# First two attention units in float32, their scales and 16-bit operands made later

## The chip, the cores and the metric

The kernel runs on one core of a Trainium2 chip. The metric is the device time of one launch in microseconds, the median of repeated runs. Five engines work side by side on the core, each through its own queue in program order: PE (TensorE, the matmuls), DVE (VectorE), ACT (ScalarE), POOL (GpSimd) and SP (SyncE, which here issues nearly all DMA transfers). They meet only through semaphores.

## The reference, cut to what matters

One transformer block with adaptive layer norm, for 2048 rows of width 512: attention with 32 query heads over 8 key and value heads of which the last 512 keys count, and then a gated feed-forward part of width 1792.

```
mod = (silu(c) @ w_mod)                                # six vectors of 512: sa, ca, ga, sb, cb, gb
h = layernorm(x) * (1 + ca) + sa
q = h @ wq                                             # 2048 x 4096, 32 heads of 128
scores = q @ k.T * 128 ** -0.5                         # 512 keys per head
o = softmax(scores) @ v
x = x + ga * (o @ wo)
h = layernorm(x) * (1 + cb) + sb
x = x + gb * ((gelu(h @ w_gate) * (h @ w_up)) @ w_down)
```

All inputs and the output are float32.

## The kernel before

**Number format.** A product of two float32 matrices is made by `mm3` (line 90) from 16-bit halves: each operand is scaled into the range of float16 and split into a high half and the low rest, and three matmuls (low by high, high by high, high by low) add up in one bank of PSUM. Each operand therefore needs a scale, which comes from norms: `sumsq` (line 218, ACT) squares a tile, `sums` (line 222, PE) adds over partitions, `norm2` takes a root on POOL (line 235), and a reciprocal on DVE closes it. `halves` (lines 158 and 159) makes high and low half on POOL, `times` (line 162) scales on POOL; `split_post` (lines 746 and 747) makes the high half on ACT and the low half on DVE.

**Units and slots.** The attention is cut into units: one head and one block of 512 queries. A unit has four slots, one for 128 queries each. In slot t the program writes, in this order: the scores of slot t on PE (`scores`, into one of two PSUM banks `ps`), their maximum on DVE (`peak`, line 989, tile `nm`), what is filed under ("e", t), the low halves of the probabilities of slot t-3 on DVE (`low`, line 1015) with their transposing DMA on SP (line 1019, `pt<-p`), what is filed under ("d", t), the exponential on ACT (`expo`, line 998, tile `ee`), the high halves of slot t-2 on ACT (line 1010), what is filed under ("x", t), then a number of tasks from a work list on PE, then what is filed under t, and what is filed under ("w", t). `at` files a step under such a key, `then` files it some slots later under ("d", ...). So a slot is a place in each queue and no time: an engine that waits in one slot holds back all that it has in later ones. In the first eight slots the number of tasks is given by hand (`EARLY`: 2, 2, 0, 0, 2, 2, 0, 0), later it is three.

**The first units.** Units 0 and 1 are heads 0 and 1 with query block 0, units 2 and 3 the same heads with block 1, and unit 4 is head 2 with block 0. Unit u's queries q are made by tasks in the slots of unit u-1 (`q_plain`, four groups of three matmuls), the probabilities of unit u meet v in the slots of unit u+2 (`pv_tasks`, tile `po`). The tasks for q of unit 4 stand at slot 12; they need the weights of pair 1 and the halves of query block 0.

**Before slot 0.** `begin` does the layer norm of the first 512 rows, makes the modulation vectors (`mod_col` on DVE, line 137, and matmuls with one column, line 1030, tile `mps`), and then the scales: `mod_scale` for the modulation vectors, `w_first` and `w_spread` for the weights of the first pair, `k_spread` for k. With these scaled vectors (`cols`) it turns the first block on PE (`ln_out`'s `turn`, line 439, tile `pln`), makes the scaled tile `hf` on DVE (line 185), sends it to DRAM (`hs<-hf`), and makes the high half on ACT (line 450) and the low half on POOL or DVE (line 454). It splits the weights (`high_w`, line 1057, `low_w`, line 1060) and k (`split_post`), and runs the q of unit 0 with matmuls on dummy data between (`q_first` and `warm`, lines 1067 and 1091). The norm statistics of the second block (`nb`, line 392) come partly in `begin`, partly in slots 0 and 1; the second block is turned in slot 2, with `hf` on DVE, high halves on ACT and low halves on POOL in slots 2 to 4.

**On POOL in slots 3 to 17.** In program order: the norm of v (line 235, `vmax`), v's halves (slot 6), the scales of weight pair 1 (`lw` to `ksc`, slots 6 to 8), its two weight tiles (`plain_steps`, slots 8 and 9), k of pair 1 (slot 10), the scales of the attention output (`ysc`, slot 12), four differences for a later block scheme (`combos`, line 581, slots 13 to 16), the product `gs` (slot 15), and the norm of the second k head (`kmax`, slot 15). DVE takes the reciprocal of that last one (line 250, `kinv`) in slot 17, ahead of the maximum of slot 18.

Of the kernel before, what the change touches and what calls it, by code (L numbers as in the profile page):

```python
# [18 lines left out]
P = 128  # L19
S, D, F = 2048, 512, 1792  # L20
HQ, HKV, DH = 32, 8, 128
W = 512
# [36 lines left out]
SETPOS = (20, 14, 13, 12, 10, 8)  # L59
SETPOS2 = (18, 12, 11, 10, 9, 7)  # L60
TAIL = 12


@with_exitstack
def block_kernel(ctx: ExitStack, tc: tile.TileContext, x, kT, v, wq, wo, wg, wu, wd, cT, wc, wm, out):
# [8 lines left out]
    def tmp(name):  # L74
        return pool.tile([P, 512], F32, tag="e", name=name, bufs=NE)
# [129 lines left out]
    def mod_scale(j, name, const_, m=None, mid=nop, between=nop):  # L205
        m, g, s = m or mod_max(j), little("mg", 2, 1), little("ms", 1, 1)
        everywhere(g, m, 2, False)
        mid()
        nc.vector.tensor_tensor(s, g[:, 0:1], g[:, 1:2], op=ALU.add)
        ts(s, s, FLOOR, RT / TOP13, ALU.max)  # L210
        ts(col(name), s, const_)
        between()
        nc.vector.reciprocal(s, s)
        ts(cols[:, j:j + 2, :], cols[:, j:j + 2, :], s)

    def sumsq(out, src):
        with nc.allow_low_precision(reason="only a scale follows from it, which the margin in norm2 covers"):
# [211 lines left out]
    def ln_out(qb, dt):  # L429
        name = (("b11", "b21"), ("y", "b22"))[qb][dt // 2]  # L430
        p = dt % 2
        st = {}

        def turn():
            st["ps"] = bank("acc", "pln", NACC)
            for i in range(QT):
                if qb and dt == 0 and i > 1:
                    fill(4)
                nc.tensor.transpose(st["ps"][:, i * P:(i + 1) * P], xn[qb * QT + i][:, dt * P:(dt + 1) * P], ident)

        def affine(act=True):
            st["f"] = pool.tile([P, D], F32, tag="ot", name="hf", bufs=NOT) if qb else tmp("hf")
            if act:
                nc.scalar.activation(st["f"], st["ps"], AF.Identity, scale=cols[:, 1, dt:dt + 1], bias=cols[:, 0, dt:dt + 1])
            else:
                ts(st["f"], st["ps"], cols[:, 1, dt:dt + 1], cols[:, 0, dt:dt + 1], op1=ALU.add)
            dma(spilled(0, qb)[:, dt, :], st["f"])

        def direct():
            nc.scalar.activation(block(0, name)[:, p, :], st["ps"], AF.Identity, scale=cols[:, 1, dt:dt + 1], bias=cols[:, 0, dt:dt + 1])  # L450

# [4 lines left out]
        return turn, affine, low, direct  # L456

    xn = {}
    waits_ = []

    def put_off(n, fn):
# [223 lines left out]
    def k_items(pr):  # L685
        g = pr // 2
        st, load = reader(kT[g])
        m = {}

        def stat():  # L690
# [12 lines left out]

        return (load, stat, spread, parts) + ((m,) if pr == 0 else ())
# [81 lines left out]
            5: ("s1", "t1"), 6: ("s2", "t2"), 7: ("s3", "t3")}  # L786
    SET, RAW = {}, {}

    def set_load(key, srcs, only=None):
        for k, src in enumerate(srcs):  # L790
            if only in (None, k):
                t = pool.tile([P, 512], F32, tag="rw", name="rw", bufs=NRW)
                dma(t, src)
                RAW.setdefault(key, {})[k] = t

# [124 lines left out]
    def q_plain(u):  # L920
# [10 lines left out]

        return [(lambda kt=kt: group(kt), (lambda: q_post(u, st["p"])) if kt == KT - 1 else None) for kt in range(KT)]

    def pv_tasks(u):
# [43 lines left out]
    def scores(t):  # L978
        u, i = divmod(t, 4)
        half, pr, qb, h = units[u]  # L980
        k = KV[half, pr, 0]
        sl = slice(i * P, (i + 1) * P)
        ps = bank("s", "ps", 2)
        mm3(ps, qT[u][:, 0, sl], qT[u][:, 1, sl], k[:, 0, :], k[:, 1, :], True, True, left=True)
        E[t] = {"ps": ps}

    def peak(t):
# [71 lines left out]
    def low_w(k):  # L1059
        nc.vector.scalar_tensor_tensor(SET[0][k][:, 1, :], RAW[0][k], col("wsc", 0), SET[0][k][:, 0, :], op0=ALU.mult, op1=ALU.subtract)  # L1060

    def q_first(warm):
        ps = bank("acc", "pq", NACC)
        for term, (a, b) in enumerate(((0, 0), (1, 0), (0, 2))):
            for kt in range(KT):
                w, m, p = SET[0][0], BK[0, ("b11", "b21")[kt // 2]], kt % 2
                nc.tensor.matmul(ps, w[:, a, kt * P:(kt + 1) * P], m[:, b + p, :], start=term + kt == 0, stop=term == 2 and kt == KT - 1)
            if term == 0:
                warm(3)
        q_post(0, ps)  # L1070

    def begin():
        now[0] = -1
        for i in range(QT):
            na[i][0]()
            na[i][1]()
        na[2][2]()
        na[3][2]()
        na[0][2]()
        na[1][2]()  # L1080
        na[2][3]()
        na[3][3]()
# [4 lines left out]
        wps = bank("s", "warm", 2)  # L1087

        def warm(n):
            for _ in range(n):  # L1090
                nc.tensor.matmul(wps, junk[:, 0:P], junk, start=True, stop=True)
# [8 lines left out]
        k0[1]()  # L1100
        ts(cols[:, 1, :], cols[:, 1, :], 1.0, None, ALU.add)
        ts(cols[:, 0, :], mps[:, 0:KT], 1.0, None, ALU.mult)
        pst = {}

        def mid():
            o0[0][0]()
            pst["w"] = sums(m["m"], 2)
            o0[1][0]()
            pst["k"] = sums(k0[4]["m"], 1)
            o0[2][0]()  # L1110
            o0[3][0]()

        mod_scale(0, "ma", SCALE * TOP13 * TOP13, mod_max(0), mid)
        w = w_first(m["m"], pst["w"])
        o0[0][1](False)
        inv_k = k0[2](False, pst["k"])
        nc.vector.reciprocal(col("wsc", 0), w)
        inv_t, last = w_spread(0, m["m"], w)
        o0[0][3]()
        high_w(0)  # L1120
        for n in range(1, KT):
            o0[n][1](False)
            o0[n][3]()
            if n == 1:
                o0[0][2](nc.gpsimd)
            if n == 2:
                inv_k()
                inv_t()
                last()
        warm(4)  # L1130
        low_w(0)
        o0[1][2]()
        o0[2][2](nc.gpsimd)
        low_k = k0[3](True)
        o0[3][2]()
        low_k()
        nb[0][0]()
        nb[0][1]()
        high_w(1)
        q_first(warm)  # L1140
        v0[1]()
        run(("e", 0))
        run(("d", 0))
        low_w(1)


    at(0, nb[0][2], nb[0][3], nb[1][0], nb[1][1], nb[2][0], nb[2][1])
# [69 lines left out]
    for g in range(NG):  # L1217
# [5 lines left out]
        spread = None if half else lambda m, pr=pr: w_spread(pr, m)  # L1223
        if 0 < g < GW:
            a, b = plain_steps(g, by)
            sched_pair(g, srcs, t0 - (19 if g > 1 else 13), spread, [(t0 - (13 if g > 1 else 8), a)], [(t0 - (11 if g > 1 else 7), b)])
# [306 lines left out]
    def pushes(u, y):  # L1533
# [305 lines left out]
```

## Time and profile before

| | us |
|---|---|
| median of 3 runs | 1733.64 (1733.24 to 1734.52) |
| the profiled execution, its own time | 1736.03 |
| its span, first to last instruction | 1734.2 |
| PE busy in the span | 1710.5 (99%) |
| DVE, ACT, POOL busy | 1430.4, 1254.9, 1093.9 |
| maximum of slot 0 (DVE) begins | 26.94 |
| maximum of slot 4 begins | 39.18 |
| maximum of slot 18 begins | 71.66 |

Times within the profile count from the start of the span. A row of the timeline gives the start, the time from the start of its first instruction to the end of its last one, the engine, the line, the operation, the tiles (written<-read), shapes and the number of instructions; in brackets stands how long the engine had been idle before it and what ended that. Matmuls follow each other faster than one lasts, so three in a row with 0.81 are not three times 0.27. A busy PE at the page's 99% includes the time in which one matmul runs out.

### The profile page before, as it was taken

To read this page: it belongs to the slowest core of one execution; us is meant where nothing else is said; L and a number is where in the kernel's file an instruction comes from. 1 tells how busy PE (TensorE), PEld (TensorE's weight loads), DVE (VectorE), ACT (ScalarE), POOL (GpSimd) and SP (SyncE) were. 2 spreads that over 40 slices of the span, in tenths; PEclk is the share of its full clock that TensorE was granted. 3 is DMA by queue.
4 is the path that set the end of the run, shared out by engine and by line. 5 is a ranking of instruction groups with operands and counts; after the bars stand their busy time and mean duration, and the time that the engine had idled before them with its cause. 6 is when DMAs were issued, how large, how long until landed. Compare 5 with 4: busy or idle time off the path is not lost.

```text
span 1734.2 us, 26336 instructions
## 1 busy us (share of the span) xinstructions
PE 1710.5 (99%) x8012; PEld 786.3 (45%) x8012; DVE 1430.4 (82%) x2476; ACT 1254.9 (72%) x2819; POOL 1093.9 (63%) x1328
## 2 busy tenths in 40 slices
PE   7999999999999999999999999999999999999998
PEld 4444444444444444444444444444444444444444
DVE  7898898888888899887788888888896788666666
ACT  5988788888888777897788777787785354455442
POOL 4889778777788884655665755747760346735424
PEclk9999999999999999999999999999999999999999
DMA  7999999999999988999999999999997556365353
GB/s 232 222 197 212 219 213 204 226 203 216 215 230 223 208 203 187 217 205 226 197 232 224 200 232 208 201 223 219 225 228 161 164 147 199 110 167 170 96 157 103
DMA packets 693454, 343.51 MB, mean 198 GB/s; under 512 B 579136, under 2 KB 602688, under 8 KB 693312
## 3 DMA queue, kind: packets, MB, share of 16 engines
q1 hardware_dynamic: 693024, 341.30, 85.7%
q8 instruction: 63, 1.03, 0.2%
q14 instruction: 79, 0.65, 0.1%
q10 hardware_dynamic: 288, 0.52, 0.1%
HBM read 137.50 MB, written 63.70 MB: 116 GB/s over the span
## 4 chain that ended last, share of the span: by engine, by line
PE 88%; DVE 4%; ACT 4%; DMA 2%; POOL 1%; issue 1%; SPq 0%; DVEq 0%; POOLq 0%; ACTq 0%
PE py L90 18%; PE po L90 17%; PE ps L90 17%; PE fa L90 8%; PE qa L90 8%; PE fc L90 4%; PE qc L90 4%; PE ya L90 3%; PE fb L90 2%; PE qb L90 2%; PE yc L90 2%; DMA pt<-p 1%; ACT ee L998 1%; ACT p L1010 1%; DVE nm L989 1%; PE pq L90 1%
## 5 line engine op out<-in xcount | busy, mean ns | idle before, releaser
L998 ACT ACTIVATE ee<-ps,nm 128x512 f32<-128x512 f32 x512 | 349.7, 683 | 186.1 <-DVE nm L989 181.0
L1015 DVE SCALAR_TENSOR_TENSOR p<-ee,rr,p 128x512 f16<-128x512 f32 x512 | 456.7, 892 | 6.2 <-ACT p L1010 5.8
L989 DVE TENSOR_REDUCE nm<-ps 128x1 f32<-128x512 f32 x512 | 350.1, 684 | 106.6 <-PE ps L90 104.0
L90 PE MATMUL ps<-k,qt 128*128 128x512 f16 x1536 | 414.8, 379 | 5.3 <-ACT ee L998 4.1
L1010 ACT ACTIVATE p<-ee,rr 128x512 f16<-128x512 f32 x512 | 364.5, 712 | 21.0 <-DMA pt<-p 10.0
L90 PE MATMUL po<-pt,v 128*128 128x512 f16 x1536 | 373.0, 379 | 2.8 <-DMA pt<-p 1.8
L90 PE MATMUL py<-wo,ot 128*128 128x512 f16 x1536 | 371.5, 379 | 0.0
L90 PEld LDWEIGHTS <-w 128*128 128x128 f16 x2184 | 213.4, 98 | 258.8 <-issue 0.8
L90 PEld LDWEIGHTS <-v 128*128 128x128 f16 x1536 | 149.8, 98 | 185.5 <-DMA pt<-p 3.5
L90 PEld LDWEIGHTS <-ot 128*128 128x128 f16 x1536 | 150.2, 98 | 181.7 <-DVE ot L747 0.5
L90 PEld LDWEIGHTS <-qt 128*128 128x128 f16 x1536 | 145.7, 98 | 176.4 <-issue 5.0
L1319 POOL TENSOR_TENSOR fg<-fg 128x512 f32<-128x512 f32 x48 | 62.9, 1310 | 148.5 <-DVE fg L1293 145.6
L747 DVE SCALAR_TENSOR_TENSOR ot<-po,ot 128x512 f16<-128x512 f32 x128 | 87.7, 685 | 37.5 <-ACT ot L746 37.0
L1303 ACT ACTIVATE at<-fg 128x512 f16<-128x512 f32 x92 | 56.4, 626 | 83.7 <-DVE fg L1293 63.6
L998 ACT ACTIVATION_READ_ACCUMULATOR ee<-ps,nm 128x1 f32 x512 | 99.9, 195 | 0.0
L959 DVE SCALAR_TENSOR_TENSOR acc<-py,ysc,acc 128x512 f32<-128x512 f32 x128 | 94.6, 739 | 5.3 <-PE py L90 5.3
L90 PE MATMUL qa<-t,w 128*128 128x512 f16 x348 | 84.9, 379 | 0.0
L235 POOL TENSOR_TENSOR lw<-lw,half__86 128x1 f32<-128x1 f32 x39 | 24.0, 616 | 92.4 <-DVE lw L185 92.4
L90 PE MATMUL fa<-t,w 128*128 128x512 f16 x336 | 81.6, 379 | 0.0
L746 ACT ACTIVATE ot<-po 128x512 f16<-128x512 f32 x128 | 73.7, 576 | 5.0 <-PE po L90 5.0
L90 PEld LDWEIGHTS <-wo 128*128 128x128 f16 x504 | 49.3, 98 | 61.0 <-issue 2.0
L90 PE MATMUL ya<-at,wo 128*128 128x512 f16 x288 | 76.0, 379 | 0.9 <-DVE yt L1686 0.7
(243 smaller groups left out, 2765.5 us busy)
## 6 DMA issues: line engine op xcount, KB each, us to landing
w<-kept SPq DMA_DIRECT2D x123, 256.0 KB, 3.4
wo<-kept SPq DMA_DIRECT2D x72, 256.0 KB, 3.3
kept<-stage SPq DMA_DIRECT2D x67, 256.0 KB, 3.3
raw<-in_wo SPq DMA_DIRECT2D x56, 256.0 KB, 3.2
kept<-w SPq DMA_DIRECT2D x39, 256.0 KB, 3.4
rw<-in_wq SPq DMA_DIRECT2D x38, 256.0 KB, 3.1
hs<-hf SPq DMA_DIRECT2D x32, 256.0 KB, 2.8
pt<-p SPq DMA_TRANSPOSE x512, 3.5
```

The costliest lines, as they stand in the source:

```text
L90: nc.tensor.matmul(ps, a, b, start=first and n == 0, stop=last and n == 2, skip_group_check=chain)
L235: nc.gpsimd.tensor_tensor(out, out, half_, op=ALU.pow)
L746: nc.scalar.activation(t[:, 0, :], src, AF.Copy, scale=scale)
L747: return lambda: nc.vector.scalar_tensor_tensor(t[:, 1, :], src, scale, t[:, 0, :], op0=ALU.mult, op1=ALU.subtract)
L959: nc.vector.scalar_tensor_tensor(acc[ti], st["p"], by, acc[ti], op0=ALU.mult, op1=ALU.add)
L989: nc.vector.tensor_reduce(nm, E[t]["ps"], axis=AX.X, op=ALU.max, negate=True)
L998: nc.scalar.activation(e, E[t]["ps"], AF.Exp, bias=E[t]["nm"], scale=1.0, accum_out=sm[:, t % 2:t % 2 + 1])
L1010: nc.scalar.activation(p16[:, 0, :], E[t]["e"], AF.Copy, scale=E[t]["r"])
L1015: nc.vector.scalar_tensor_tensor(p16[:, 1, :], E[t]["e"], E[t]["r"], p16[:, 0, :], op0=ALU.mult, op1=ALU.subtract)
L1303: nc.scalar.activation(t[:, 0, :], g, AF.Copy)
L1319: nc.gpsimd.tensor_tensor(g[o], g[a], g[b], op=ALU.subtract)
```

## The change

- `q_full` replaces `q_first` for unit 0 and `q_plain` for unit 1: four float32 matmuls of 128x512 each from the weight tile as loaded (`RAW[0]`) and the unscaled `hf` tiles of the first block, kept in `HF`. ACT copies the result into one float32 tile with the factor 128 ** -0.5.
- `scores` of units 0 and 1 (`NFULL = 2`, slots 0 to 7) is one float32 matmul with the k tile as loaded.
- `begin` no longer makes any scale or half. It turns the first block, makes `hf` on DVE and ACT by turns, takes the statistics of three tiles of the second block, and runs q of unit 0. The dummy matmuls of `warm` go.
- The scales (`mod_scale`, `w_first`, `k_spread`, `w_spread`) are made in slots 0 to 2; the halves of the first weights in slots 1 to 3 (ACT high, DVE low), those of k in slots 4 and 5.
- The first block's `hf` are multiplied by the scale on POOL and sent to DRAM in slots 4 and 5 (`scaled`); their high and low halves are made on POOL in slots 5, 7, 8 and 9 (`both`).
- Loads move: pair 1's weights are loaded in slot 1 into the tag "wo"; the loads of two of the four tiles for the first `combos` group move from slots 1 and 2 to slots 7 and 8.

```diff
+NFULL = 2
...
         def affine(act=True):
-            st["f"] = pool.tile([P, D], F32, tag="ot", name="hf", bufs=NOT) if qb else tmp("hf")
+            st["f"] = pool.tile([P, D], F32, tag="ot", name="hf", bufs=NOT)
...
+            if qb:
+                dma(spilled(0, qb)[:, dt, :], st["f"])
+            else:
+                HF[dt] = st["f"]
+
+        def scaled(by):
+            times(st["f"], by)
             dma(spilled(0, qb)[:, dt, :], st["f"])
+
+        def both():
+            t = block(0, name)
+            nc.gpsimd.tensor_scalar(t[:, p, :], st["f"], 1.0, 1.0, op0=ALU.mult, op1=ALU.mult)
+            nc.gpsimd.tensor_tensor(t[:, 2 + p, :], st["f"], t[:, p, :], op=ALU.subtract)
...
+    def q_full(u):
+        st = {}
+
+        def group(kt):
+            if kt == 0:
+                st["p"] = bank("acc", "pq", NACC)
+            nc.tensor.matmul(st["p"], RAW[0][u][:, kt * P:(kt + 1) * P], HF[kt], start=kt == 0, stop=kt == KT - 1)
+
+        def post():
+            qT[u] = pool.tile([P, QB], F32, tag="qt", name="qf", bufs=3)
+            nc.scalar.activation(qT[u], st["p"], AF.Copy, scale=SCALE)
...
     def scores(t):
...
-        mm3(ps, qT[u][:, 0, sl], qT[u][:, 1, sl], k[:, 0, :], k[:, 1, :], True, True, left=True)
+        if u < NFULL:
+            nc.tensor.matmul(ps, qT[u][:, sl], KV["raw"], start=True, stop=True)
+        else:
+            k = KV[half, pr, 0]
+            mm3(ps, qT[u][:, 0, sl], qT[u][:, 1, sl], k[:, 0, :], k[:, 1, :], True, True, left=True)
...
     def begin():
...
+        for n in range(KT):
+            o0[n][0]()
+            o0[n][1](n % 2 == 1)
+        for i in range(3):
+            nb[i][0]()
+            nb[i][1]()
+        mm = mod_max(0)
+        k0[1]()
         v0[1]()
-        run(("e", 0))
-        run(("d", 0))
-        low_w(1)
...
+        for go, post in q_full(0):
...
+        pw, pk = sums(m["m"], 2), sums(k0[4]["m"], 1)
+        box = {}
+
+        def scales():
+            box["h"] = mod_scale(0, "ma", SCALE * TOP13 * TOP13, mm)
+            w = w_first(m["m"], pw)
+            inv_k = k0[2](False, pk)
+            inv_t, last = w_spread(0, m["m"], w)
+            at(("e", 1), lambda: nc.vector.reciprocal(col("wsc", 0), w))
+            at(("e", 2), inv_k, inv_t, last)
+
+        at(("e", 0), scales)
+        at(("x", 1), lambda: high_w(0))
+        at(("d", 2), lambda: low_w(0))
+        at(("x", 2), lambda: high_w(1))
+        at(("d", 3), lambda: low_w(1))
+        low_k = []
+        at(("x", 4), lambda: low_k.append(k0[3](True)))
+        at(("d", 5), lambda: low_k[0]())
+        for n, t in zip(range(KT), (4, 4, 5, 5)):
+            at(t, lambda n=n: o0[n][4](box["h"]))
+        for n, t in zip(range(KT), (5, 7, 8, 9)):
+            at(t, o0[n][5])
...
-                at(base + ((0, 0, 0, 2)[k] if p else (-10, -2, -1, -9)[k]), load)
+                at(base + ((0, 0, 0, 2)[k] if p else (-4, -2, -1, -3)[k]), load)
...
+                at(1, lambda srcs=srcs: set_load(1, srcs, tag=("wo", 8)))
...
+                at(("w", 8), a)
+                at(("w", 9), b)
...
-            w = q_plain(u + 1) if 0 < u + 1 < 4 * GW else []
+            w = (q_full if u + 1 < NFULL else q_plain)(u + 1) if 0 < u + 1 < 4 * GW else []
```

More of the change, by code (lines that the diff above doesn't have):

```diff
@@ L214, in mod_scale @@
         ts(cols[:, j:j + 2, :], cols[:, j:j + 2, :], s)
+        return s
     def sumsq(out, src):
@@ L454, in low @@
             eng.tensor_tensor(t[:, 2 + p, :], st["f"], t[:, p, :], op=ALU.subtract)
-        return turn, affine, low, direct
-    xn = {}
+        return turn, affine, low, direct, scaled, both
+    xn, HF = {}, {}
     waits_ = []
@@ L688, in k_items, with load @@
         m = {}
+        if pr == 0:
+            def load():
+                st["r"] = KV["raw"] = pool.tile([P, W], F32, tag="wo", name="kr", bufs=8)
+                dma(st["r"], kT[g])
         def stat():
@@ L787, in block_kernel, with set_load @@
     SET, RAW = {}, {}
-    def set_load(key, srcs, only=None):
+    def set_load(key, srcs, only=None, tag=("rw", NRW)):
         for k, src in enumerate(srcs):
             if only in (None, k):
-                t = pool.tile([P, 512], F32, tag="rw", name="rw", bufs=NRW)
+                t = pool.tile([P, 512], F32, tag=tag[0], name="rw", bufs=tag[1])
                 dma(t, src)
@@ L932, in q_plain @@
         return [(lambda kt=kt: group(kt), (lambda: q_post(u, st["p"])) if kt == KT - 1 else None) for kt in range(KT)]
+    def q_full(u):
[7 more added lines that the diff above has]
+            nc.scalar.activation(qT[u], st["p"], AF.Copy, scale=SCALE)
+        return [(lambda kt=kt: group(kt), post if kt == KT - 1 else None) for kt in range(KT)]
     def pv_tasks(u):
@@ L980, in scores @@
         half, pr, qb, h = units[u]
-        k = KV[half, pr, 0]
         sl = slice(i * P, (i + 1) * P)
         ps = bank("s", "ps", 2)
-        mm3(ps, qT[u][:, 0, sl], qT[u][:, 1, sl], k[:, 0, :], k[:, 1, :], True, True, left=True)
+        if u < NFULL:
[3 more added lines that the diff above has]
+            mm3(ps, qT[u][:, 0, sl], qT[u][:, 1, sl], k[:, 0, :], k[:, 1, :], True, True, left=True)
         E[t] = {"ps": ps}
@@ L1060, in low_w @@
         nc.vector.scalar_tensor_tensor(SET[0][k][:, 1, :], RAW[0][k], col("wsc", 0), SET[0][k][:, 0, :], op0=ALU.mult, op1=ALU.subtract)
[L1062 to L1070, printed above, removed]
     def begin():
@@ L1086, in begin @@
         mps = bank("s", "mps", 2)
[L1087 to L1091, printed above, removed]
         for dt in range(KT):
@@ L1099, in begin @@
         pair_stat(0, m, 1)
-        k0[1]()
         ts(cols[:, 1, :], cols[:, 1, :], 1.0, None, ALU.add)
         ts(cols[:, 0, :], mps[:, 0:KT], 1.0, None, ALU.mult)
[L1103 to L1140, printed above, removed]
-        v0[1]()
-        run(("e", 0))
-        run(("d", 0))
-        low_w(1)
-    at(0, nb[0][2], nb[0][3], nb[1][0], nb[1][1], nb[2][0], nb[2][1])
+        for n in range(KT):
[6 more added lines that the diff above has]
+        k0[1]()
@@ new lines, in begin @@
+        v0[1]()
+        for go, post in q_full(0):
+            go()
+            if post:
+                post()
+        pw, pk = sums(m["m"], 2), sums(k0[4]["m"], 1)
[7 more added lines that the diff above has]
+            at(("e", 2), inv_k, inv_t, last)
@@ new lines, in begin @@
+        at(("e", 0), scales)
[10 more added lines that the diff above has]
+            at(t, o0[n][5])
+    at(0, nb[0][2], nb[0][3])
@@ L1225, in block_kernel @@
             a, b = plain_steps(g, by)
-            sched_pair(g, srcs, t0 - (19 if g > 1 else 13), spread, [(t0 - (13 if g > 1 else 8), a)], [(t0 - (11 if g > 1 else 7), b)])
+            if g > 1:
+                sched_pair(g, srcs, t0 - 19, spread, [(t0 - 13, a)], [(t0 - 11, b)])
+            else:
+                m1 = {}
+                at(1, lambda srcs=srcs: set_load(1, srcs, tag=("wo", 8)))
+                at(("w", 3), lambda: pair_stat(1, m1, 0))
+                at(("w", 4), lambda: pair_stat(1, m1, 1))
+                at(("w", 6), lambda spread=spread: spread(m1["m"]))
+                at(("w", 8), a)
+                at(("w", 9), b)
         elif g >= GW and (not half or pr < GW):
```

## The prediction

> **What bounds the kernel now.** I read the page, then the busy times by stretch, then the timeline from 13 to 80 us engine by engine, then the waits.
>
> ```profile
> PE 1710.5 (99%) x8012; PEld 786.3 (45%) x8012; DVE 1430.4 (82%) x2476; ACT 1254.9 (72%) x2819; POOL 1093.9 (63%) x1328
> 90.00:100.00 10.00, 8.04 (x37) 3.32 (x35) 9.77 (x15) 9.17 (x25) 7.76 (x6) 1.00 1.03 209
> 120.00:140.00 20.00, 20.00 (x94) 9.11 (x93) 16.23 (x27) 15.60 (x38) 18.91 (x20) 1.00 0.74 164
> PE ps L90 <- ACT ee L998: 3.7, 4, 1.4
> 72.50:97.50 25.00, 22.78 (x55) 1.00 1.02 215
> ```
>
> PE is full from about 100 us on (20.00 of 20.00 in the third line; the second, just before, has 8.04 of 10). From there PE's order is fixed and its work nearly untouched, so the end moves by what PE's position at about 100 us moves. Before that, PE is not the limit: in the 32 us from 68 us on it waits 3.7 us for exponentials (fourth line), while ACT alone is busy 22.78 of 25.00 us (fifth line, ACT's busy time from 72.5 to 97.5). So slots 18 to 27 go at ACT's pace, and whatever delays slot 18 is carried to 100 us and to the end. The change must be judged by when slot 18 starts.
>
> What ends the wait ahead of slot 18 now:
>
> ```profile
> 41.90 0.19 POOL L239 TENSOR_SCALAR lw<-vmax 128x1 f32<-128x1 f32 x1
> 43.16 0.69 POOL L162 TENSOR_SCALAR raw<-raw,vsc 128x512 f32<-128x512 f32 x1 [1.06 <-DVE vsc L720]
> 43.94 0.62 POOL L158 TENSOR_SCALAR v<-raw 128x512 f16<-128x512 f32 x1
> 44.64 1.15 POOL L159 TENSOR_TENSOR v<-raw,v 128x512 f16<-128x512 f32 x1
> 46.55 0.55 POOL L235 TENSOR_TENSOR lw<-lw,half__86 128x1 f32<-128x1 f32 x1 [0.76 <-DVE lw L185]
> 52.29 1.16 POOL L159 TENSOR_TENSOR w<-rw,w 128x512 f16<-128x512 f32 x1
> 60.37 0.23 POOL L239 TENSOR_SCALAR ysc<-ysc 128x1 f32<-128x1 f32 x1 [1.07 <-DVE ysc L233]
> 67.70 0.26 POOL L239 TENSOR_SCALAR ysc<-ysc,vmax 128x1 f32<-128x1 f32 x1 [2.58 <-DVE kmax L183]
> 71.36 0.19 POOL L239 TENSOR_SCALAR kmax<-kmax 128x1 f32<-128x1 f32 x1
> 71.58 0.16 DVE L250 RECIPROCAL kinv<-kmax 128x1 f32<-128x1 f32 x1 [0.74 <-POOL kmax L239]
> ```
>
> DVE stands idle 0.74 us until POOL has `kmax`, and the maximum of slot 18 is next in DVE's queue. POOL thus already decides slot 18 by a hair. From the end of v's norm (42.09) to the end of `kmax` (71.55) are 29.46 us, of which POOL waits 1.06 + 0.76 + 1.07 + 2.58 = 5.47. Its queue there is worth 24.0 us with the small steps between instructions.
>
> **The start.** Rows of PE, ACT and DVE:
>
> ```profile
> 12.77 0.99 PE L1030 MATMUL mps<-silu,wct 128*128 128x1 f32 x4
> L439 PE MATMUL pln<-ident,xn 128*128 128x128 f32 x16 | 3.8, 424 | 0.0
> 18.32 1.57 PE L1091 MATMUL warm<-junk 128*128 128x512 f16 x4
> 19.72 0.81 PE L1067 MATMUL pq<-b,w 128*128 128x512 f16 x3
> 33.98 1.64 PE L439 MATMUL pln<-ident,xb 128*128 128x128 f32 x13 [0.58 <-DVE xb L413]
> 24.77 0.69 ACT L746 ACTIVATE qt<-pq,qsc 128x512 f16<-128x512 f32 x1 [0.43 <-PE pq L1067]
> 26.94 0.68 DVE L989 TENSOR_REDUCE nm<-ps 128x1 f32<-128x512 f32 x1
> ```
>
> The modulation matmuls end at 13.76 and stay. The 16 transposes then need no scale: 3.8 us, to 17.6, the next matmul at 17.4. The `hf` tiles follow on DVE and ACT one behind the other (0.8 us each, row at 34.35 below), the last at about 18.4, in time for the fourth matmul of q.
>
> No row has a float32 matmul of 512 columns. Low end: at 33.98 a float32 transpose of 128 columns takes 1.64/13 = 0.13, four times that is 0.5. High end: all four products of 16-bit halves at the 1.57/4 = 0.39 of the first dummies, 1.6. I take four times the earlier transposes' 3.8/16 = 0.24, so 0.95, since q runs right behind them. Float16 matmuls go at about 0.22 once fast ((0.81 less a tail of 0.16) / 3), so a set of three is 0.65. Then: q of unit 0 is 4 x 0.95 = 3.8, to 21.4 with its tail; the copy 0.7, to 22.2; the scores 0.95 and a tail, to 23.4. The maximum of slot 0 starts at 23.4 in place of 26.94: **3.5 us won.** The `sumsq` steps and three norm statistics (3 us of DVE) lie beside q and cost nothing; ACT has them done before q ends.
>
> The Trainium skill, page "FP8 and Floating Point Precision", section TensorE Precision Notes, gives a true FP32 matmul four passes; by the float16 row that is an estimate of 0.86 at the full clock and twice that at half. Its page "TensorE: Matmul & The Clock Gate" (Part 4) holds that transposes do not raise the clock; the dummies' 0.39 after 3.8 us of transposes agrees. With the dummies gone, that speaks for the high end; it is the third rival.
>
> **What slots 0 to 3 get.**
>
> ```profile
> 14.94 0.42 DVE L198 TENSOR_REDUCE mg<-pst 128x2 f32<-128x256 f32 x1 [0.78 <-PE pst L196]
> 16.43 0.80 DVE L185 TENSOR_SCALAR hf<-pln,cols 128x512 f32<-128x512 f32 x1
> 17.16 0.15 DVE L183 TENSOR_SCALAR kmax<-pst 128x1 f32<-128x1 f32 x1
> 17.52 0.16 DVE L1117 RECIPROCAL wsc<-lw 128x1 f32<-128x1 f32 x1 [0.22 <-POOL lw L239]
> 20.52 0.84 DVE L1060 SCALAR_TENSOR_TENSOR w<-rw,wsc,w 128x512 f16<-128x512 f32 x1
> 27.55 0.68 DVE L392 BATCH_NORM_STATS2 bn<-acc 128x6 f32<-128x512 f32 x1
> 29.55 0.68 DVE L989 TENSOR_REDUCE nm<-ps 128x1 f32<-128x512 f32 x1
> 32.07 0.68 DVE L989 TENSOR_REDUCE nm<-ps 128x1 f32<-128x512 f32 x1
> 32.67 0.74 DVE L747 SCALAR_TENSOR_TENSOR qt<-pq,qsc,qt 128x512 f16<-128x512 f32 x1
> 34.35 1.53 DVE L185 TENSOR_SCALAR hf<-pln,cols 128x512 f32<-128x512 f32 x2 [0.42 <-PE pln L439]
> 36.30 0.69 DVE L989 TENSOR_REDUCE nm<-ps 128x1 f32<-128x512 f32 x1 [0.43 <-PE pst L222]
> 39.18 0.67 DVE L989 TENSOR_REDUCE nm<-ps 128x1 f32<-128x512 f32 x1
> ```
>
> From maximum 0 to maximum 4 are now 39.18 - 26.94 = 12.24 us, nearly all of it DVE's own work. After the change:
> - Slot 0 (now 2.61): two statistics (27.55 to 29.55, 2.0) go, the chain of the scales (14.94 to 16.43, 1.5, and 0.15 for `kmax`) comes. But PE has two float32 groups of q before the next scores: 0.2 for the scale's transposes + 2 x 0.95 + 0.95 = 3.1, and that ends last.
> - Slot 1 (2.52): a reciprocal of 0.16 more; PE again 2 x 0.95 + 0.95 with a tail, 3.0.
> - Slot 2 (4.23): q's low half (0.7) goes, two reciprocals (0.3) and the weights' low half (0.8) come, and the scores of slot 3, behind the transposes as now, take 0.3 more: 4.9.
> - Slot 3 (2.88): the second weights' low half, 0.75: 3.65.
>
> Together 14.65, so 2.4 of the 3.5 are given back and **1.1 us is left at slot 4**. ACT's added high halves fit into its idle time there. Later float32 scores (0.3 each in slots 4 to 7) and k's low half fall where POOL decides, and are charged nothing; if POOL doesn't decide they take the remaining 1.1.
>
> **What POOL gets.**
>
> ```profile
> L158 POOL TENSOR_SCALAR w<-rw 128x512 f16<-128x512 f32 x50 | 41.4, 827 | 3.5
> L159 POOL TENSOR_TENSOR w<-rw,w 128x512 f16<-128x512 f32 x50 | 63.4, 1267 | 4.2
> L162 POOL TENSOR_SCALAR rw<-rw,wsc 128x512 f32<-128x512 f32 x34 | 24.9, 731 | 13.5 <-DMA rw<-in_wq 13.5
> 56.62 2.11 PE L90 MATMUL pq<-b,w 128*128 128x512 f16 x9
> 41.16 1.45 SPq L1019 DMA_TRANSPOSE pt<-p  x1
> 17.27 3.68 SPq L96 DMA_DIRECT2D hs<-hf  x4
> ```
>
> Four `scaled` at 0.73 and four `both` at 0.83 + 1.27, with 0.09 between instructions (43.16 + 0.69 = 43.85, the next starts at 43.94), make 4 x 0.82 + 4 x 2.28 = **12.4 us** of POOL, all between the end of v's norm and `kmax`. What it used to do for this block lay before slot 0, so nothing leaves these slots. The 5.47 us of waits take up part. v's norm ends at 42.09 - 1.1 = 41.0; then 24.0 + 12.4 without a pause ends `kmax` at **77.4 in place of 71.55, 5.85 later**. DVE's reciprocal in slot 17 waits for it, behind that the maximum of slot 18, behind that ACT's exponential and PE's scores of slot 20.
>
> On the way there is an earlier wait of the same kind: q of unit 4 (56.62, slot 12) needs the first weight tile of pair 1, whose low half now ends at 53.45. Ahead of it come all `scaled` and three `both` (10.1 us) against 1.82 of waits: 53.45 + 10.1 - 1.8 - 1.1 = 60.6, so PE waits 4 us in slot 12. That is inside the 5.85, as the later wait covers it. After `kmax` POOL's order is as before and all of it moves along.
>
> On SP the four spills (now at 17.27) stand in slots 4 and 5 between the transposing DMAs of slots 1 to 3 (the one of slot 1 is now at 41.16) and wait for POOL's `scaled`, done at 42.6 and 44.3. Behind them are the transposes for slots 2 and 3 and their readers, the matmuls with v from slot 8. That costs 0 to 1 us in slots that POOL holds back by more: I take 0. The moved loads are wanted only in slots 13 on.
>
> **Sum.** Profiled execution: its own time is 1736.03, 1.8 of it outside the span and untouched, so 1736.03 + 5.8 = 1741.8. The median of the runs shown lies 2.4 below that execution: 1733.64 + 5.8 = **1739.4**.
>
> **The rivals.** About 0.2% (3.5 us) is what a measurement of this kernel can tell from no change.
> - *The start decides (faster).* The 3.5 us of the start go through to 100 us. For: DVE has idle time before 26.94 that the statistics fill, and PE's order after slot 4 is the same. Against: POOL's 12.4 us against 5.47 of waits. It decides from the point where POOL's added work stays below those waits plus what is won at slot 4. At 0.95 per float32 matmul that gives 1733.64 - 3.5 = 1730.1; at 0.5 q ends with the last `hf` at 19.1, maximum 0 comes at 20.5, 6.4 are won: 1727.2. Chance 0.11.
> - *A draw.* POOL's eight steps run at the shortest rows (0.69, 0.62 and 1.15: 10.9 us) and slots 0 to 3 keep the gain: 42.09 - 3.5 + 24.0 + 10.9 = 73.5, 1.9 later, 1735.5. Chance 0.2.
> - *Half the clock.* float32 matmuls at 1.6 us: q to 24.1, copy to 24.9, scores to 26.9; nothing is won, the 2.4 of slots 0 to 3 are lost, `kmax` ends at 42.09 + 2.4 + 36.4 = 80.9, 9.3 later: 1743.0. Chance 0.12.
> - *The forecast.* Chance 0.57, own range 1737.2 to 1742.
>
> **How the numbers follow.** Slower by over 0.2% is the forecast and half the clock: 0.69. Within 0.2% the draw, 0.2. Faster 0.11. The range leaves out the first rival and stretches to the third with one more microsecond for SP: 1732 to 1744.
>
> **What would show it.** Right: maximum 0 near 23.4 and maximum 4 near 38; POOL without a wait from about 41 to 77; PE idle some 4 us ahead of q of unit 4; DVE idle 2 us or more ahead of `kinv`; maximum 18 near 77.5. Wrong: maximum 18 before 73.5; POOL with waits between slots 4 and 17; float32 matmuls below 0.5 or above 1.2; PE not full at 110 us.

## The result and the profile after

| | before | after |
|---|---|---|
| median of 5 runs, us | 1734.52 (1733.24 to 1736.56) | 1741.50 (1740.15 to 1741.83) |
| profiled execution, its own time | 1736.03 | 1740.15 |
| its span | 1734.2 | 1738.4 |

The ratio of the runs is 1.0038, with a 95% interval of 1.0027 to 1.0050: the changed kernel is slower by 6.6 us (4.7 to 8.7). The medians lie 7.0 us apart. The two profiled executions lie only 4.2 us apart in their spans: the one of the changed kernel is the fastest of its five runs, the one of before lies 1.5 us above the median of its five. The predicted 5.8 us stands between.

From the page after, the line of the engines and the chain of work that ended last, then a row of the busy times by stretch (start and end, length, busy us of PE, weight load, DVE, ACT and POOL, granted clock, DMA share, GB/s), which shows whether PE is full:

```profile
PE 1712.1 (98%) x7989; PEld 787.2 (45%) x7989; DVE 1433.1 (82%) x2472; ACT 1254.5 (72%) x2817; POOL 1105.5 (64%) x1341
PE 88%; DVE 3%; POOL 3%; ACT 3%; issue 1%; DMA 1%; SPq 0%; POOLq 0%; DVEq 0%; ACTq 0%
110.00:140.00 30.00, 30.00 (x143) 13.55 (x142) 27.12 (x49) 23.99 (x57) 25.94 (x34) 1.00 0.83 182
```

POOL has 11.6 us more work (1093.9 before), and PE is full from 110 us on, as before. So the end again stands where PE stood near 110 us.

The start, from the timelines of PE and DVE:

```profile
11.79 0.99 PE L1065 MATMUL mps<-silu,wct 128*128 128x1 f32 x4
12.65 3.37 PE L441 MATMUL pln<-ident,xn 128*128 128x128 f32 x16
15.86 3.60 PE L958 MATMUL pq<-hf,rw 128*128 128x512 f32 x8
20.14 1.13 PE L1016 MATMUL ps<-kr,qf 128*128 128x512 f32 x2 [0.66 <-ACT qf L962]
...
21.30 0.69 DVE L1024 TENSOR_REDUCE nm<-ps 128x1 f32<-128x512 f32 x1 [1.78 <-PE ps L1016]
...
36.38 0.67 DVE L1024 TENSOR_REDUCE nm<-ps 128x1 f32<-128x512 f32 x1
```

The maximum of slot 0 comes at 21.30 instead of 26.94, that of slot 4 at 36.38 instead of 39.18. A lead of 5.6 us has become 2.8.

Then POOL, from the end of v's norm to `kmax`, and DVE's reciprocal and the maximum of slot 18 behind it; the last line is that maximum in the kernel before:

```profile
39.12 0.19 POOL L241 TENSOR_SCALAR lw<-vmax 128x1 f32<-128x1 f32 x1
39.40 3.55 POOL L163 TENSOR_SCALAR hf<-hf,ms 128x512 f32<-128x512 f32 x4
...
57.39 1.59 POOL L160 TENSOR_TENSOR w<-rw,w 128x512 f16<-128x512 f32 x1
...
75.85 0.19 POOL L241 TENSOR_SCALAR kmax<-kmax 128x1 f32<-128x1 f32 x1
...
76.07 0.16 DVE L252 RECIPROCAL kinv<-kmax 128x1 f32<-128x1 f32 x1 [2.89 <-POOL kmax L241]
76.15 0.67 DVE L1024 TENSOR_REDUCE nm<-ps 128x1 f32<-128x512 f32 x1
```

```profile
71.66 0.67 DVE L989 TENSOR_REDUCE nm<-ps 128x1 f32<-128x512 f32 x1
```

No row of POOL between the first and the fourth carries a bracket: it never waits for 36.7 us, where before it waited four times. DVE stands 2.89 us for `kmax` (0.74 before), and behind that comes the maximum of slot 18, at 76.15 instead of 71.66. PE's own waits, from its timeline from 48 to 80 us:

```profile
50.14 1.46 PE L91 MATMUL po<-pt,v 128*128 128x512 f16 x6 [2.04 <-DMA pt<-p]
56.17 0.65 PE L150 MATMUL prow<-ident,cols 128*128 128x128 f32 x4 [1.18 <-DVE cols L184]
59.04 2.12 PE L91 MATMUL pq<-b,w 128*128 128x512 f16 x9 [1.57 <-POOL w L160]
62.83 1.47 PE L91 MATMUL po<-pt,v 128*128 128x512 f16 x6 [0.35 <-DMA pt<-p]
77.69 1.44 PE L91 MATMUL ps<-k,qt 128*128 128x512 f16 x3 [2.84 <-ACT ee L1033]
```

The lead is 2.1 us at slot 8 (45.56, before 47.65) and gone at slot 9 (50.77, before 49.88). What holds slot 9 is DVE, which waits twice for POOL's scales of weight pair 1 right ahead of it; before, neither reciprocal waited:

```profile
49.28 0.16 DVE L275 RECIPROCAL wsc<-lw 128x1 f32<-128x1 f32 x1 [1.84 <-POOL lw L241]
50.69 0.17 DVE L267 RECIPROCAL lr<-lt 128x1 f32<-128x1 f32 x1 [1.24 <-POOL lt L241]
50.77 0.67 DVE L1024 TENSOR_REDUCE nm<-ps 128x1 f32<-128x512 f32 x1
```

PE's waits for `cols`, which DVE makes behind these, and for POOL's weight tile follow. At slot 17 the changed kernel is 2.3 us behind (71.56, before 69.22), and DVE's longer wait for `kmax` makes that 4.5 at slot 18; the last of PE's waits comes from there. From slot 18 the distance is kept: slots 18 to 27 take 22.38 us (before 22.49), and slot 35 comes 4.50 us later than before.

### The profile page after: what moved, and what is told of

Read it like the earlier page. It is cut to its first block, busy times and chain, and to the rows that moved or that the text cites. A ratio compares the mean times of both kernels' runs of the same rounds, so it can differ in the third digit from the quotient of the medians.

```text
span 1738.4 us, 26299 instructions
## 1 busy us (share of the span) xinstructions
PE 1712.1 (98%) x7989; PEld 787.2 (45%) x7989; DVE 1433.1 (82%) x2472; ACT 1254.5 (72%) x2817; POOL 1105.5 (64%) x1341
## 4 chain that ended last, share of the span: by engine, by line
PE 88%; DVE 3%; POOL 3%; ACT 3%; issue 1%; DMA 1%; SPq 0%; POOLq 0%; DVEq 0%; ACTq 0%
PE py L91 19%; PE po L91 17%; PE ps L91 16%; PE fa L91 8%; PE qa L91 8%; PE fc L91 4%; PE qc L91 4%; PE ya L91 3%; PE fb L91 2%; PE qb L91 2%; PE yc L91 2%; DVE p L1050 1%; ACT ee L1033 1%; PE yb L91 1%; ACT p L1045 1%
## 5 line engine op out<-in xcount | busy, mean ns | idle before, releaser
L1050 DVE SCALAR_TENSOR_TENSOR p<-ee,rr,p 128x512 f16<-128x512 f32 x512 | 462.0, 902 | 6.9 <-ACT p L1045 6.7
L91 PE MATMUL ps<-k,qt 128*128 128x512 f16 x1512 | 408.9, 379 | 5.2 <-ACT ee L1033 5.1
L765 DVE SCALAR_TENSOR_TENSOR ot<-po,ot 128x512 f16<-128x512 f32 x128 | 87.7, 685 | 36.7 <-ACT ot L764 36.4
L404 POOL TENSOR_TENSOR rs<-rs,nhalf 128x1 f32<-128x1 f32 x32 | 18.5, 577 | 94.6 <-DVE rs L398 84.7
```

Source lines behind the costliest of these rows:

```text
L91: nc.tensor.matmul(ps, a, b, start=first and n == 0, stop=last and n == 2, skip_group_check=chain)
L404: nc.gpsimd.tensor_tensor(st["rs"], st["rs"], nhalf, op=ALU.pow)
L765: return lambda: nc.vector.scalar_tensor_tensor(t[:, 1, :], src, scale, t[:, 0, :], op0=ALU.mult, op1=ALU.subtract)
L1050: nc.vector.scalar_tensor_tensor(p16[:, 1, :], E[t]["e"], E[t]["r"], p16[:, 0, :], op0=ALU.mult, op1=ALU.subtract)
```

## The experiments

Start of the maximum of a slot, in us, in each profiled execution, with the span and the median of the runs. e1 to e4 ran beside a before of 1735.67 (21 runs), e6 to e10 beside one of 1735.50 (22 runs); the ratio has its 95% interval in brackets.

| kernel | slot 0 | 4 | 10 | 18 | 27 | span | median of runs, ratio to before |
|---|---|---|---|---|---|---|---|
| before | 26.94 | 39.18 | 53.28 | 71.66 | 94.15 | 1734.2 | |
| after | 21.30 | 36.38 | 53.09 | 76.15 | 98.53 | 1738.4 | 1741.50, 1.0038 [1.0027, 1.0050] |
| e1_before_pool | 26.25 | 39.86 | 56.63 | 79.75 | 102.13 | 1742.2 | 1744.03, 1.0040 [1.0028, 1.0053] |
| e2_no_pool | 22.23 | 37.30 | 53.26 | 71.91 | 94.39 | 1734.6 | 1736.58, 1.0003 [0.9994, 1.0012] |
| e3_no_lows | 22.07 | 37.16 | 53.42 | 72.66 | 95.14 | 1734.8 | 1738.51, 1.0016 [1.0007, 1.0024] |
| e4_defer | 21.65 | 36.73 | 53.58 | 73.40 | 99.83 | 1747.9 | 1750.66, 1.0082 [1.0068, 1.0095] |
| e6_early | 21.39 | 36.91 | 54.10 | 75.54 | 97.93 | 1737.7 | 1739.92, 1.0028 [1.0018, 1.0038] |
| e8_early_defer3 | 22.24 | 37.76 | 53.80 | 73.16 | 98.25 | 1738.8 | 1740.60, 1.0032 [1.0019, 1.0045] |
| e9_no_pool_early | 23.17 | 38.25 | 52.70 | 71.44 | 93.94 | 1733.7 | 1736.22, 1.0003 [0.9995, 1.0012] |
| e10_early_dve_lows | 22.33 | 37.85 | 54.08 | 74.84 | 97.33 | 1738.1 | 1739.79, 1.0027 [1.0017, 1.0038] |

The theory is that POOL's added queue sets `kmax`, and `kmax` sets slot 18. The rivals are the start's own cost (float32 matmuls and DVE in slots 0 to 7) and the transfers that moved into slots 4 and 5.

**POOL's work alone, put into the kernel before.**

```diff
+    dum, dum16 = two tiles of their own
+    for t_ in (4, 4, 5, 5): at(t_, like_scaled)   # POOL: dum = dum * half * 1
+    for t_ in (5, 7, 8, 9): at(t_, like_both)     # POOL: high half, then subtraction
```

> The kernel before with eight dummy steps on POOL alone, on tiles of their own, in the slots and of the kinds of the change (four of 128x512 float32 to float32 in slots 4, 4, 5, 5; four pairs float32 to float16 and subtraction in slots 5, 7, 8, 9). Theory (POOL's queue decides slot 18): the norm of the second k head ends at 42.1 + 24.0 + 12.4 = 78.5 in place of 71.55, the maximum of slot 18 starts near 78.5 in place of 71.66, the run is 6 to 7 us slower than before. Rival (float32 matmuls and DVE's added work in slots 0 to 7): no change within 1 us. Rival (the spills and loads moved into slots 4 to 8 hold back the transposing DMAs): no change within 1 us.

```profile
42.58 0.19 POOL L239 TENSOR_SCALAR lw<-vmax 128x1 f32<-128x1 f32 x1
...
79.45 0.19 POOL L239 TENSOR_SCALAR kmax<-kmax 128x1 f32<-128x1 f32 x1
```

From v's norm to `kmax` are 36.9 us, against 36.7 in the changed kernel and 29.5 before. By the ratio the run is 6.9 us above the kernel before (4.9 to 9.2), by the medians 8.4, by the profiled spans 8.0: eight steps whose results nobody reads cost as much as the whole change. As in the changed kernel, POOL's debt shows before slot 18: DVE waits 2.54 and 1.24 us for the scales of weight pair 1 ahead of slot 9, which comes 4.6 us late (54.45, before 49.88). The theory holds, and in the spans the start of the change pays part of this back (8.0 here, 4.2 there).

**The change without POOL's work.**

```diff
-            times(st["f"], by)
             dma(spilled(0, qb)[:, dt, :], st["f"])
-            at(t, o0[n][5])
+            at(t, nop)
```

> The changed kernel without the eight POOL steps: the first block's hf are spilled unscaled and its 16-bit halves are zeros, written before slot 0. All float32 matmuls, DVE steps and transfers stay. Theory: POOL has its old queue from a start 2.8 us earlier, the maximum of slot 18 starts between 69 and 71, the run is 0 to 3 us faster than before, 6 to 9 faster than the changed kernel. Rival (float32 and DVE): still 4 to 7 us slower than before. Rival (transfers): PE still waits some 2 us for a transposing DMA at about 50 us, still 3 or more slower than before.

```profile
15.89 4.48 PE L957 MATMUL pq<-hf,rw 128*128 128x512 f32 x8
...
50.32 1.46 PE L91 MATMUL po<-pt,v 128*128 128x512 f16 x6 [1.35 <-DMA pt<-p]
```

The loss goes, as the theory says. But no gain stays either: a draw, where 0 to 3 us faster had been expected. The lead is 4.7 us at slot 0, 1.9 at slot 4, nothing at slot 10; slot 18 comes at 71.91, where 69 to 71 had been expected. So the start's gain is lost in slots 0 to 9 without any help from POOL, part of it in PE's wait for a transposing DMA at 50.32.

**The change without the four subtractions on POOL.**

```diff
             nc.gpsimd.tensor_scalar(t[:, p, :], st["f"], 1.0, 1.0, ...)
-            nc.gpsimd.tensor_tensor(t[:, 2 + p, :], st["f"], t[:, p, :], op=ALU.subtract)
```

> The changed kernel without the four subtractions on POOL (the low halves of the first block are zeros, written before slot 0). Theory: 4 x 1.24 + 0.36 = 5.3 us leave POOL's queue, the norm of the second k head ends near 70.8 in place of 76.04, the maximum of slot 18 near 72, the run is within 1.5 us of before. Rival (float32 and DVE) and rival (transfers): as the changed kernel, 4 to 7 us slower than before.

`kmax` ends at 72.54 (70.8 expected), slot 18 stands at 72.66 (72 expected). 4.9 us out of the queue move `kmax` by 3.5: in this execution v's norm ends 0.8 us later (40.08), and POOL waits again, 0.91 us for DVE ahead of `kmax`. The profiled execution is 0.6 us above that of before, the runs 2.8 (1.2 to 4.2), more than the 1.5 expected. Together with the run before it this grades the cause: all eight steps +6.6, without the subtractions +2.8, without any +0.5 (in the spans +4.2, +0.6 and +0.4).

**Moving other POOL work behind `kmax`: the first group of differences six slots later.**

```diff
-CB = (11, 27)
+CB = (17, 27)
```

> The changed kernel, nothing left out, with the differences of the first block scheme filed six slots later (17 in place of 11), so that three of them (1.27, 1.60 and 1.27 us) stand behind the norm of the second k head in POOL's queue. Theory: that norm ends near 71.8, DVE has its own work until 73.2 there, the maximum of slot 18 starts at 73.2 in place of 76.15, the run is 2.5 to 3 us faster than the changed kernel and 1 to 2 slower than before. Rivals: no change against the changed kernel, except up to 1 us from two loads that move out of slots 7 and 8.

This missed by 10 us and more: by the ratio the run is 14.2 us above the kernel before, where 1 to 2 had been expected (3.6 to 4.1, if 2.5 to 3 are taken off the changed kernel's 6.6). Slot 18 came at 73.40, as expected; but 2.7 us were gone again by slot 25, and slot 34 came at 125.11 instead of 115.36. PE, SP's queue and POOL there:

```profile
121.04 2.72 PE L91 MATMUL po<-pt,v 128*128 128x512 f16 x6 [6.69 <-DMA pt<-p]
```

```profile
116.84 0.33 SPq L97 DMA_DIRECT2D u<-hs  x1
117.27 1.23 SPq L1054 DMA_TRANSPOSE pt<-p  x1
```

```profile
105.82 1.27 POOL L595 TENSOR_TENSOR cb<-cb 128x512 f32<-128x512 f32 x1 [6.46 <-DMA cb<-hs]
...
115.22 1.60 POOL L385 TENSOR_TENSOR t<-u,t 128x512 f16<-128x512 f32 x1
```

The first group's last subtraction ends at 116.82. The second group's load `u<-hs` needs that tile and goes out on SP at 116.84, and the transposing DMA that PE waits for stands behind it on SP. POOL's own wait of 6.46 us for a load had made it later still. The first group had been pushed into the slots in which the second begins. So a load that waits for its tile held back the transfers behind it on the same queue: SP issued nothing from 108.36 to 116.84.

**The scalings two slots earlier.**

```diff
-        for n, t in zip(range(KT), (4, 4, 5, 5)):
+        for n, t in zip(range(KT), (2, 2, 3, 3)):
             at(t, lambda n=n: o0[n][4](box["h"]))
```

> The changed kernel with the four in-place scalings of the first block's tiles (and the spills that go out with them) in slots 2, 2, 3, 3 instead of 4, 4, 5, 5; nothing left out. In the changed kernel POOL had pauses between 29.8 and 36.6 us and none from 39.4 to 76.0. Theory (POOL's queue after v's norm sets `kmax`, and with it slot 18): the 3.55 us of scalings leave the full stretch, `kmax` ends near 72.8 instead of 76.04, the maximum of slot 18 stands near 73 instead of 76.15, the run is 2 to 3.5 us faster than the changed kernel. Second cause, transfers: the spills go out before the transposing DMAs of slots 2 and 3, so that PE's wait of 2.2 us near 50 us (for slot 3's transposed probabilities) shrinks under 1. Rival (the loss is in the float32 matmuls and the unscaled path of slots 0 to 3): neither moves, slot 18 stays near 76 and the run within 1 us of the changed kernel. Against it could stand that POOL's work in slots 2 and 3 slows DVE there: then the maximum of slot 4 comes later than 36.4.

A miss: slot 18 gained 0.6 us and not 3, and the run is 4.9 us above before by the ratio (3.1 to 6.6), against 6.6 for the changed kernel, which these intervals do not tell apart.

```profile
33.81 2.23 POOL L163 TENSOR_SCALAR hf<-hf,ms 128x512 f32<-128x512 f32 x2
...
39.65 0.19 POOL L241 TENSOR_SCALAR lw<-vmax 128x1 f32<-128x1 f32 x1
39.94 1.79 POOL L163 TENSOR_SCALAR hf<-hf,ms 128x512 f32<-128x512 f32 x2
...
75.24 0.19 POOL L241 TENSOR_SCALAR kmax<-kmax 128x1 f32<-128x1 f32 x1
```

```profile
30.70 5.69 SPq L97 DMA_DIRECT2D hs<-hf  x4
36.48 1.40 SPq L1054 DMA_TRANSPOSE pt<-p  x1
...
40.66 1.42 SPq L97 DMA_DIRECT2D hs<-hf  x2
42.17 1.29 SPq L1054 DMA_TRANSPOSE pt<-p  x1
```

Only two of the four scalings left the full stretch; the two of slot 3 stand in POOL's queue behind v's norm all the same. And SP fared worse: its spills wait there for POOL, and slot 1's transposing DMA starts at 42.17, against 38.36 in the changed kernel. PE's wait near 50 us became 2.5 us (2.04 in the changed kernel) and did not shrink.

**The same, and the first group of differences three slots later** (`CB = (14, 27)`).

> The changed kernel with the scalings and spills in slots 2, 2, 3, 3 and, besides, the first group of differences three slots later (base 14 instead of 11), so that three of its 128x512 operations (1.27 + 1.60 + 1.27 = 4.1 us) no longer stand ahead of `kmax` on POOL; its subtractions of low halves then fall into slots 25 to 28, ahead of the second group's loads. Nothing left out. Theory: POOL's queue ends `kmax` 3.3 + 4.1 us earlier than 76.04, near 69 to 70 (where its input from PE and DVE comes last), DVE has no wait ahead of `kinv`, the maximum of slot 18 stands at 71 to 72.5, and the run, unless the later differences cost something in slots 20 to 30 as they did when put six slots later (there 2.7 us were gone by slot 25), is 4 to 6 us faster than the changed kernel: 1734 to 1738. Rival (slots 18 on are held by something other than POOL's queue): the run no better than the one with early scalings alone.

```profile
72.11 0.19 POOL L241 TENSOR_SCALAR kmax<-kmax 128x1 f32<-128x1 f32 x1
```

`kmax` ends 3.7 us earlier than in the changed kernel (69 to 70 had been expected) and slot 18 comes 3.0 earlier, at 73.16; DVE no longer waits for `kmax` there. At slot 27 only 0.3 of that is left, and the run is no faster than with the early scalings alone. Where it went shows in the groups of DVE's rows from 77 to 104 us (count, busy us, mean ns), first in the changed kernel, then here:

```profile
L1050 DVE SCALAR_TENSOR_TENSOR p<-ee,rr,p 128x512 f16<-128x512 f32 x12 | 12.5, 1040 | 0.0
L765 DVE SCALAR_TENSOR_TENSOR k<-raw,ksc,k 128x512 f16<-128x512 f32 x1 | 1.1, 1093 | 0.0
```

```profile
L1050 DVE SCALAR_TENSOR_TENSOR p<-ee,rr,p 128x512 f16<-128x512 f32 x11 | 13.2, 1200 | 0.2 <-ACT p L1045 0.2
L765 DVE SCALAR_TENSOR_TENSOR k<-raw,ksc,k 128x512 f16<-128x512 f32 x1 | 1.8, 1753 | 0.0
```

DVE is busy 26.0 and 26.1 of these 27 us, so its time is the time of these slots, and the same instructions have become longer: 11 x 0.16 + 0.66 = 2.4 us, most of the 2.7 lost. They ran beside POOL's postponed differences. That POOL's work stretches DVE's is read from these rows, not tried by itself. The Trainium skill, page "GPSIMD Engine Reference", section 8 (Key points), says that the two share their ways into SBUF and get into each other's way when DVE reads two inputs from there. The trace agrees: both instructions above read two tiles in SBUF, while DVE's maximum, which reads one in PSUM, kept its mean (679 ns in the changed kernel, 677 here).

**No POOL work, and the spills two slots earlier.** As e2_no_pool, with the spills in slots 2, 2, 3, 3.

> As the run without POOL's eight added operations (unscaled spills; the first block's halves are zeros written ahead of slot 0, so its output differs), but with the four spills of the first block in slots 2, 2, 3, 3 instead of 4, 4, 5, 5. It asks what ate the start's gain between slots 4 and 10 there, where the maxima stood at 37.30 (slot 4), 48.52 (9), 53.26 (10) and 71.91 (18). Theory (transfers): the spills stood on SP ahead of slot 2's and 3's transposing DMAs, for which PE waited 1.5 us near 50.3; with the spills earlier that wait falls under 0.7, slot 9 stands near 47.5, slot 10 near 52 to 52.5, slot 18 near 71, and the run is 0.5 to 1.5 us faster than that one (1735 to 1736). Rival (the gain is eaten by the longer slots 0 to 3 and by ACT and DVE, which are full there): slots 9 to 18 as in that run within 0.4, the run the same.

PE's wait near 50 us is gone. Slot 4 was 0.95 us later than in e2_no_pool, and slot 9 still is (49.47, where 47.5 had been expected); but slot 10 comes at 52.70, earlier than there. From slot 4 to slot 10 it takes 14.45 us instead of 15.96: the spills ahead of the transposes cost 1.5 us there, as this run's theory says. The run, at 1736.22 against 1736.58 where 0.5 to 1.5 us less had been expected, can't be told from that one.

**Earlier scalings, and the subtractions on DVE.**

```diff
-            nc.gpsimd.tensor_tensor(t[:, 2 + p, :], st["f"], t[:, p, :], op=ALU.subtract)
+            at(("d", now[0] + 3), lambda: nc.vector.tensor_tensor(t[:, 2 + p, :], ...))
```

with the high halves in slots 4 to 7 and the scalings in 2, 2, 3, 3.

> The changed kernel with the scalings and spills in slots 2, 2, 3, 3, the four rounded high halves of the first block on POOL in slots 4 to 7, and the four subtractions for the low halves on DVE in slots 7 to 10 (DVE was busy 3.7 of 7 us from 46 to 53 and 6.0 of 7 from 53 to 60 in the changed kernel); nothing left out. Theory (POOL's queue): after v's norm POOL has 3.6 us of scalings and 5 us of subtractions less than in the changed kernel, its queue no longer decides, `kmax` ends near 70 to 71.5 (its input comes last), slot 18 stands at 71 to 72.5, PE no longer waits for pair 1's first weight tile near 59, and the run is at the level of the kernel before or up to 2 us under it: 1733 to 1736.5. Rival (DVE decides slots 4 to 10 already): four subtractions of 0.7 to 1.2 us on DVE push slots 7 to 12 back by 2 to 4 us, and the run stays near the changed kernel or above it.

```profile
70.86 0.27 POOL L241 TENSOR_SCALAR ysc<-ysc,vmax 128x1 f32<-128x1 f32 x1 [2.58 <-DVE kmax L184]
```

```profile
46.00:53.00 7.00, 5.45 (x33) 3.31 (x32) 5.95 (x11) 4.94 (x14) 6.58 (x10) 1.00 1.02 253
53.00:60.00 7.00, 5.74 (x31) 2.86 (x31) 6.69 (x11) 5.26 (x15) 6.56 (x9) 1.00 1.06 216
```

POOL waits again ahead of `kmax`, as before the change, so its queue no longer decides; but DVE now works 12.6 of these 14 us (9.8 in the changed kernel), slot 12 comes at 61.60 (59.49 in the changed kernel), `kmax` ends at 74.73 (70 to 71.5 expected), and the run stays at 1739.8. The rival named for this run was right about the time, and slot 8, with a subtraction right ahead of it, comes at 48.69 (45.56 in the changed kernel). But 1.5 us of such delays stand already at slot 4 (37.85, there 36.38), and from slot 4 to slot 12 it takes 23.75 us instead of 23.11: the subtractions stand where DVE waited for POOL in the changed kernel. No version beat the kernel before.

## Why the prediction was right

The time was predicted as before + 5.8, 1739.4 us on the median of three runs then shown; the runs give + 6.6 (4.7 to 8.7) and 1741.50, the profiled executions + 4.2. The mechanism was right: POOL, without a pause, sets slot 18, and slot 18 is carried to the end. Some of the closeness is luck, as the third step and the last paragraph say. Step by step:

- **The start: 3.5 us predicted, 5.64 won.** 1.0 of the difference is the end of the modulation matmuls at 12.78 instead of 13.76. Most of that need not be the change's doing: the moment differs between executions, and the unchanged start in e1_before_pool has it at 13.06 and slot 0 at 26.25 instead of 26.94. The rest is the transposes, q starting 3.1 us behind the modulation matmuls where 3.6 was computed, and the float32 matmul: 3.60 us for four of them with their tail, 0.86 each from the spacing of the records, where 0.95 was taken, over q and the first scores.
- **Slots 0 to 3: 14.65 predicted, 15.08 measured.** Slots 0 and 1 were a little cheaper than computed (2.80 and 2.58 for 3.1 and 3.0), slots 2 and 3 dearer (5.26 and 4.44 for 4.9 and 3.65). Left at slot 4: 2.8, predicted 1.1.
- **POOL: v's norm at 41.0 predicted, 39.31 measured; the queue 36.4 predicted, 36.7 measured; `kmax` at 77.4 predicted, 76.04 measured.** This is the step that carries the forecast. Its sum held within 0.3 us, and e1_before_pool gives nearly the same, 36.9, without the rest of the change. That it held so closely is partly luck, since two errors cancel: the eight added steps took 11.2 us of the queue instead of 12.4 (from start to start of the rows: 3.5 for the scalings, then 2.2 and three times 1.8), and the rest took 25.5 instead of 24.0, with single steps longer than before, such as v's scaling at 1.12 instead of 0.69. The 1.4 us by which `kmax` was early is the better start, 1.7, less that 0.3.
- **PE's wait for the weight tile: 4 us predicted, 1.6 measured** (the row at 59.04). The tile came at 58.98, not 60.6, and PE had lost 2.0 and 1.2 us in two waits before, which the prediction did not have. Nor did it have the first place at which POOL's debt arrives: slot 9, where DVE waits 1.84 and 1.24 us for POOL's scales. The later wait for `kmax` covers all of these, as it said.
- **SP: 0 taken, at most 1 allowed; PE waited 2.0 us.** The bound of this term was too small. The end did not feel it, because POOL held slot 9 back, and slot 18 by more; without POOL's work it is 1.5 us at slot 10 (e2_no_pool against e9_no_pool_early), and still not seen in the runs.
- **Carried to the end:** 4.49 at slot 18, 4.38 at slot 27, 4.50 at slot 35, 4.2 at the end. The prediction named ACT as what these slots go by; from 77 to 104 us DVE is the fuller one (26.0 of 27 us, ACT 24.6), and in e8_early_defer3 these slots took longer as DVE's instructions did. The conclusion, that slot 18 is carried, was the same.

*The start decides* fails twice: POOL takes more than the start gives, and without POOL's work (e2_no_pool) the gain is gone at slot 10 as well. *A draw* is what the change is without POOL's eight steps. *Half the clock* did not occur in the profiled execution, where the eight records of q follow each other 0.43 us apart; but the row of e2_no_pool above has 4.48 us for the same eight, and e9_no_pool_early 4.92, the first ones 0.85 apart. In those executions the slow matmuls cost 0.9 and 1.3 us of the start, and the one that lost more reached slot 18 the earlier, with its spills out earlier too.

That 5.8 lies so near the 6.6 of the runs is luck in part as well. In the profiled executions, the only ones that show the steps, `kmax` came 4.5 us later and not 5.85. Their pair understates the difference of the medians by 2.9 us (1.51 by which before's lies above its median, 1.35 by which the changed kernel's lies below its own). The end of the modulation matmuls is 1.0 of it at most; what makes up the rest stays open. So does how much DVE's stretching costs by itself, since no run took POOL's differences away alone.

## What to carry to other kernels

Work taken off the critical start has to be put somewhere: count it on the engine that gets it, up to the next place where that engine releases someone, and compare it with that engine's waits up to there (12.4 us computed and 11.2 measured, against 5.5 here). Moving such a debt elsewhere only helps where there is room to pay it: two slots earlier it held up SP's queue, on DVE it came into slots where DVE worked 12.6 of 14 us, three slots later it seems to have stretched DVE, and six slots later it ran into the next group and cost some 8 us more than the change itself. A gain of several microseconds at the start is worth what is left of it at the first place where another engine or a transfer comes last; here that was nothing.

## What the hardware showed

- The float32 matmul of 128x512 stands in the trace as two records. At their fastest they are 0.43 us apart (eight in 3.60 us with a tail of 0.16), so one matmul is 0.86. The Trainium skill, page "FP8 and Floating Point Precision", section TensorE Precision Notes, gives a true float32 matmul four passes. The trace agrees: four times the float16 matmul's 0.216 (three in 0.81 with that tail) is 0.86.
- With the same code up to there, PE's matmuls get twice as fast at different moments. In the changed kernel q was fast from its start at 15.86, behind 16 transposes and, from 5.73 to 12.78, matmuls with one column; in e2_no_pool and e9_no_pool_early, with the same transposes, the first records of q were 0.85 us apart, twice the 0.43. The granted clock in the profile's rows does not show it: it stands at 1.00 there in all three. The Trainium skill, page "TensorE: Matmul & The Clock Gate", Part 4, holds that transposes do not raise the clock. The latter two cases fit that; in the first, the transposes or the one-column matmuls ahead of them may have raised it, and no run here settles which.
- In PE's pause of 3 us ahead of 77.69 the granted clock fell to half, for 3.4 us:

```profile
77.03:80.45 3.42, 2.76 (x7) 1.01 (x7) 3.40 (x9) 3.39 (x9) 3.05 (x7) 0.50 0.36 77
```

No cost shows: DVE and ACT work 3.40 and 3.39 of these 3.42 us, and slots 18 to 27 take no longer than before (22.38 us, before 22.49).
